# Softcap attention and a maxout MLP: the multiply by the softmax reciprocals of quads 5 to 23, on VectorE in one operation in place of two on GpSimd

## The chip, the cores and the metric

One Trainium2 chip, one core. The time is that of the device for one execution, in microseconds (us), lower is better. A core has five engines with queues of their own, each in order: TensorE (PE, with its weight loads as PEld), VectorE (DVE), ScalarE (ACT), GpSimd (POOL) and SyncE (SP), which here issues almost all DMAs. Engines wait for each other through semaphores. SBUF is the working memory, PSUM takes the results of matmuls.

## The reference

Attention with a soft cap for 8 batches, 12 heads, 448 positions and head size 64, then a layer that takes the larger of two projections, and an output projection. Inputs and output are fp32.

```python
scores = (1 / np.sqrt(64)) * np.matmul(q, k.transpose(0, 1, 3, 2))
scores = cap * np.tanh(scores / cap)                     # cap = 30
attn = np.exp(scores - np.max(scores, axis=-1, keepdims=True))
attn = attn / (np.sum(attn, axis=-1, keepdims=True) + 1e-09)
x = np.matmul(attn, v)                                   # [8, 12, 448, 64]
x = x.transpose(0, 2, 1, 3).reshape(8 * 448, 768)
out = np.maximum(x @ w1, x @ w2) @ w_out                 # w1, w2: 768x1024, w_out: 1024x768
```

## The kernel before

**Attention.** The work is cut into pairs of heads (48, six to a batch) and *quads* of two pairs (24, `t` = 0 to 23 in the main loop). Keys lie across the partitions, so the scores come out transposed: for each quad PE makes 14 score matmuls (`scores`, L295 and L290), ACT makes tanh (L296, L298) and exp (L303, `ex`). No maximum is subtracted; the cap bounds the scores. `pv` (L339, L353) multiplies by v for one pair and accumulates in the PSUM tile pv, of which there is one buffer; VectorE copies it to U (L356, four buffers, one per quad). For the sums over keys VectorE first adds the parts of exp (esum: `add`, L322, L324, L326), from quad 5 on, and PE sums over partitions with a matrix of ones (L352) into ss, copied to st (L359).

**The reciprocals.** They go round through DRAM, to be turned and copied to all partitions. For quad t: SP stores the sums (`sums<-st`, L362) right after pv of the second pair of quad t; VectorE takes the reciprocal (`invert`, L368) and SP writes it to DRAM (`rec_d<-rec_s`, L370) one quad later; SP reads it back for 64 partitions at a time (`spread`, `rec_b<-rec_d`, L376, two DMAs, two buffers) two quads later. `normalize` (L388) then multiplies U by rec_b, an operation for each pair on GpSimd, and writes bf16 to xT, which holds two batches.

**The MLP.** The larger of two projections is computed as relu(x @ (w1 - w2)) + x @ w2; the second part is multiplied through beforehand (wm = w2 @ w_out). `moe(b)` is a generator for one batch. PE makes eight groups of six matmuls (L401), each into a buffer of the PSUM tile mm (two buffers for all of this work); VectorE drains each with a relu to gT (L405). Then come output halves of 14 matmuls (L413 with wm, L416 with w_out), drained to osb (L420) and stored by SP (L431, L436, L440, L423). `F(n)` takes n matmuls out of the queue `fill_q`, to fill PE between attention's matmuls. In the first quads the queue holds the preparation of the weights; moe(0) is appended in quad 4, moe(1) to moe(6) in quads 8, 11, 14, 17, 20 and 23, and moe(7) after the loop.

**Order.** All of it is written by hand: an engine runs its instructions in the order in which the program issues them. In quad t of the loop, from quad 5 on, the order around `normalize` is: scores and exp for quad t+1, filling, `cross` (a DMA that transposes q and k of three pairs, `qkT<-kqf`, L268, in two of three quads), `spread(t - 2)`, loads of q, k and v; `pv(t, 0)`, filling; **`normalize(t - 2)`**; more scores, esum additions and filling; `invert(t - 1)`, loads; the last scores of t+1; `pv(t, 1)` with its copies and the store of the sums. GpSimd's other work in the loop is to cast the loaded q, k and v (L178 to L190, L158, L163). After the loop there are `invert`, `spread` and `normalize` for the last two quads between stretches of filling.

The lines of the helper that the quads call:

Of the kernel before, what the change touches and what calls it, by code (L numbers as in the profile page):

```python
# [10 lines left out]
def kernel(  # L11
# [11 lines left out]
    nc = tc.nc  # L23
# [14 lines left out]
    NQ = N // 2  # L38
# [174 lines left out]
    def subtract(c):  # L213
        nc.vector.tensor_sub(wd_sb[:, c, :], w1_in[c], w2b[:, c, :])
# [35 lines left out]
    def transposes(i):  # L250

        g, n = divmod(i, L)
        ps = mm_psum.tile([P, 512], f32, name="mm").bitcast(bf16)
        x = flat(g)[:, n, :]

        todo = [(j * D, (j % 3) * P + (j // 3) * 64) for j in range(6)]
        odd = i // NP % 2
        todo += [(Q0 + j * D, Q0 + (64 * j if not odd else 0 if j == 6 else 64 + 64 * j)) for j in range(R7)]
        for c, to in todo:
            for a in range(2):  # L260
                r = slice(64 * a, 64 * a + 64)
                nc.tensor.transpose(ps[r, to : to + 64], x[r, c : c + D], ident[r, r])
        nc.tensor.transpose(ps[:, NJ * P : Q0], x[:, NJ * P : Q0], ident)
        nc.vector.tensor_copy(qkT_of(g)[:, n, :, :].rearrange("p j c -> p (j c)")[:, : Q0 + S], ps[:, : Q0 + S])  # L264

    def cross(g):

        nc.sync.dma_start_transpose(  # L268
            out=qkT_of(g).rearrange("p n j c -> p (n j) c"), in_=kqf[g % 2].rearrange("p n j c -> p (n j c)")
        )  # L270
# [6 lines left out]
    def scores(t, p, m0=0, m1=2):  # L277

        if m0 == 0:
            tanh[t, p] = att.tile([P, 4, S], bf16, name="tanh")  # L280
        if p == 2:
            s = s_psum.tile([P, 2, 512], f32, name="s")
        for m, (ab, j) in list(enumerate(PARTS[p]))[m0:m1]:
            i = 2 * t + ab
            g = i // L
            k0 = qkT[g][:, i % L, :, :].rearrange("p j c -> p (j c)")
            o = Q0 + (64 * (i // NP % 2) if g >= NT else 0)
            qTn = k0[:, o : o + S]
            if p == 2:
                nc.tensor.matmul(s[:, m, :S], k0[:, 3 * P : 4 * P], qTn)  # L290
                continue
            s = s_psum.tile([P, 2, 512], f32, name="s")
            for h in range(2):
                r = slice(64 * h, 64 * h + 64)
                nc.tensor.matmul(s[:, h, :S], k0[r, j * P : (j + 1) * P], qTn[r, :])  # L295
            nc.scalar.activation(tanh[t, p][:, 2 * m : 2 * m + 2, :], s[:, :, :S], AF.Tanh, scale=scale / cap)  # L296
        if p == 2:
            nc.scalar.activation(tanh[t, p][:, 0:2, :], s[:, :, :S], AF.Tanh, scale=scale / cap)  # L298

    def ex(t, p):  # L300
        n = 2 if p == 2 else 4
        expo[t, p] = att.tile([P, n, S], bf16, name=f"expo{p}", bufs=1 if p == 3 else 2)
        nc.scalar.activation(expo[t, p], tanh[t, p][:, 0:n, :], AF.Exp, scale=float(cap))  # L303
# [7 lines left out]
    def add(t, ab, step):  # L311

        if t < NS or t >= NQ:
            return
        if t not in esum:
            esum[t] = att.tile([P, 4, S], bf16, name="esum")
        d = esum[t][:, 2 * ab : 2 * ab + 2, :]
        if step == 2:

            r = slice(64 * ab, 64 * ab + 64)  # L320
            d = esum[t][r, ab::2, :]
            nc.vector.tensor_add(d, d, expo[t, 2][r, :, :])  # L322
        elif step == 0:
            nc.vector.tensor_add(d, e_of(t, ab, 1 if ab else 0), e_of(t, ab, 2 if ab else 1))  # L324
        else:
            nc.vector.tensor_add(d, d, e_of(t, ab, 0 if ab else 2))  # L326

    U, sums, rec, recd = {}, {}, {}, {}
# [37 lines left out]
    def invert(t):  # L366
        r = xpool.tile([32, 56], f32, name="rec_s")
        nc.vector.reciprocal(r, sums[t])  # L368
        recd[t] = dram.tile([32, 56], f32, name="rec_d")
        nc.sync.dma_start(out=recd[t], in_=r)  # L370

    def spread(t):
        rec[t] = xpool.tile([P, 2, S], f32, name="rec_b")
        lines = recd[t].rearrange("(n h a) c -> h n (a c)", h=2, a=8)
        for h in range(2):
            nc.sync.dma_start(  # L376
                out=rec[t][64 * h : 64 * h + 64, :, :], in_=lines[h : h + 1, :, :].to_broadcast([64, 2, S])
            )

    xT = {}  # L380

    def normalize(t, ab, eng=nc.gpsimd):
        i = 2 * t + ab
        b, hp = divmod(i, NP)
        if i % (2 * NP) == 0:
            xT[b // 2] = xpool.tile([P, NP, 2 * S], bf16, name="xT")
        cs = slice((b % 2) * S, (b % 2 + 1) * S)
        eng.tensor_mul(xT[b // 2][:, hp, cs], U[t][:, ab, :], rec[t][:, ab, :])  # L388


    gT = {}
# [52 lines left out]
    def F(n):  # L444
        while n > 0 and fill_q:
            try:
                next(fill_q[0])
                n -= 1
            except StopIteration:
                fill_q.pop(0)  # L450
# [68 lines left out]
    def weights(i):  # L519
        if MS <= i < MS + KC:  # L520
            fill_q.append(turn_w2(i - MS))
        if MS < i <= MS + KC:
            fill_q.append(premultiply(i - MS - 1))

    def extra(i):
        for f, a in todo[i]:
            f(*a)

    for t in range(NQ):
        i = 2 * t  # L530
        more = t + 1 < NQ
        more8 = 1 if t >= 8 and more else 0
        weights(i)
        if t % 3 == 2 and t > 5:
            fill_q.append(moe(t // 3 - 1))
        if more:
            scores(t + 1, 0)
        ex(t, 3)
        F(2)
        if 3 < i <= 3 + KC:  # L540
            subtract(i - 4)
        add(t, 0, 1)
        F(2)
        if i + 3 < NT * L:
            transposes(i + 3)
        if t == 0:
            cast(nc.vector, 0, "v")
        F(4 + more8 if more else 0)
        if t == 4:
            normalize(t - 2, 0)  # L550
            normalize(t - 2, 1)
        if t in crosses:
            cross(crosses[t])
        if t > 4:
            spread(t - 2)
        extra(i)
        F(5 + 2 * more8 if more else 3)
        if more:
            scores(t + 1, 1)
            ex(t + 1, 0)  # L560
        if t > 0:
            pv(t, 0)
        F(4)
        add(t, 1, 0)
        F(3 + more8 if more else 4)
        F(3 if more else 0)
        if 3 <= i < 3 + KC:
            subtract(i - 3)
        if t > 4:
            normalize(t - 2, 0)  # L570
            normalize(t - 2, 1)
        if more:
            scores(t + 1, 2)
            ex(t + 1, 1)
        weights(i + 1)
        if t == 4:
            fill_q.append(moe(0))
        if i + 4 < NT * L:
            transposes(i + 4)
        add(t, 0, 2)  # L580
        F(2 + more8 if more else 2)
        add(t, 1, 2)
        F(4 + more8 if more else 3)
        add(t, 1, 1)
        F(2 if more else 8)
        if 1 < t < 4:
            spread(t - 2)
        if t > 2:
            invert(t - 1)
        extra(i + 1)  # L590
        F(2 + more8 if more else 0)
        if more:
            scores(t + 1, 3)
            ex(t + 1, 2)
        if t == 0:
            pv(t, 0)
        if t == 3:
            spread(t - 1)
        pv(t, 1)
        F(4)  # L600
        if more:
            add(t + 1, 0, 0)
        F(3 if more else 0)
        if 0 < t < 3:
            invert(t - 1)
        if 1 < t < 4:
            normalize(t - 2, 0)
            normalize(t - 2, 1)
    F(6)
    spread(NQ - 2)  # L610
    F(10)
    invert(NQ - 1)
    F(16)
    spread(NQ - 1)
    normalize(NQ - 2, 0)
    normalize(NQ - 2, 1)
    F(30)
    normalize(NQ - 1, 0)
    normalize(NQ - 1, 1)
    fill_q.append(moe(B - 1))  # L620
    F(10 ** 9)
# [33 lines left out]
```

## Time and profile before

| | |
|---|---|
| time, median of 3 runs | 374.17 us (371.63 to 374.65) |
| the profiled execution | 374.65 us, span 372.9 us, PE clock 0.995 |
| busy: PE, ACT, DVE, POOL | 344.8, 281.5, 231.5, 161.5 us |
| L388, the multiplies on POOL | 48, 59.4 us, mean 1258 ns, idle before them 125.5 us |
| DMA | 71.56 MB, mean 192 GB/s |

The span runs from the first to the last instruction. The page cuts it into 40 slices of 9.3 us; a digit is the busy share of a slice in tenths. In lists of waits, "A <- B: x, n, m" says that A's engine stood x us in all, n times and m us at the longest, until B was done. In a timeline row the first number is the start in us and the second how long the row took; in brackets stands the idle time before it and what ended it. SPq is SP issuing a DMA. "x2" are two instructions merged in one row.

### The profile page before, as it was taken

The numbers are of one execution on the slowest core, as the hardware profiler recorded it, in microseconds if no ns is written. First come the engines' busy times: TensorE is split into PE (matmuls) and PEld (weight loads), VectorE is DVE, ScalarE is ACT, GpSimd is POOL, SyncE is SP. The second block draws the span as 40 slices with busy tenths as digits, with TensorE's granted clock in tenths as the row PEclk, the third lists the DMA queues.
The fourth block names the chain that finished last, engine by engine and source line by source line (L and its number), as shares of the span: only waits on it lengthen the run. The fifth ranks groups of instructions, "written<-read, shape, count | busy, mean of one in ns | idle before, by whom it ended". The sixth has DMA issues, their size and how long they took to land.

```text
span 372.9 us, 6501 instructions
## 1 busy us (share of the span) xinstructions
PE 344.8 (92%) x2454; PEld 165.2 (44%) x2454; DVE 231.5 (62%) x389; ACT 281.5 (75%) x265; POOL 161.5 (43%) x197
## 2 busy tenths in 40 slices
PE   4668897999999999999979999999999999999996
PEld 2223444444444444444434344534453445555553
DVE  4153557577886777767674687659767868533421
ACT  4996998899999989998978899988998993000000
POOL 4851168690864376234554554544644332220000
PEclk9999999999999999999998999999999999999999
DMA  7998899768799979999599968897998133512022
GB/s 260 327 241 186 324 274 274 149 145 189 190 238 238 212 188 252 202 209 251 145 230 239 261 189 193 220 235 214 216 261 200 53 92 129 150 45 86 0 86 84
DMA packets 101200, 71.56 MB, mean 192 GB/s; under 512 B 56496, under 2 KB 96176, under 8 KB 101168
## 3 DMA queue, kind: packets, MB, share of 16 engines
q1 hardware_dynamic: 99216, 67.99, 70.6%
q0 software_dynamic: 1952, 3.15, 4.6%
q8 instruction: 19, 0.31, 0.4%
q14 instruction: 13, 0.11, 0.1%
HBM read 53.48 MB, written 11.18 MB: 173 GB/s over the span
## 4 chain that ended last, share of the span: by engine, by line
PE 56%; ACT 15%; DMA 12%; DVE 8%; SPq 5%; issue 2%; POOL 2%; DVEq 0%; POOLq 0%; ACTq 0%
PE mm L416 14%; PE mm L401 12%; PE mm L413 10%; ACT expo L303 7%; ACT tanh L296 7%; PE pv L339 6%; PE s L295 5%; DMA qr<-in_q_dram 4%; DMA kr<-in_k_dram 3%; PE pv L353 3%; DMA qkT<-kqf 2%; PE ss L352 2%; PE mm L232 2%; DMA vr<-in_v_dram 1%; DMA rec_d<-rec_s 1%
## 5 line engine op out<-in xcount | busy, mean ns | idle before, releaser
L303 ACT ACTIVATE expo<-tanh 128x1792 bf16<-128x1792 bf16 (+1 forms) x96 | 144.8, 1509 | 0.1
L296 ACT ACTIVATE tanh<-s 128x896 bf16<-128x896 f32 x144 | 124.2, 915 | 26.1 <-PE s L295 24.6
L388 POOL TENSOR_TENSOR xT<-u,rec_b 128x448 bf16<-128x448 f32 x48 | 59.4, 1258 | 125.5 <-DMA rec_b<-rec_d 81.0
L416 PE MATMUL mm<-wo_sb,gT 128*128 128x384 bf16 x448 | 86.1, 328 | 0.0
L401 PE MATMUL mm<-xT,wd_sb 128*128 128x448 bf16 x384 | 79.3, 352 | 1.0 <-DVE osb L420 0.6
L356 DVE COPY u<-pv 128x448 f32<-128x448 f32 x48 | 30.0, 624 | 72.0 <-PE pv L353 70.5
L413 PE MATMUL mm<-wm_sb,xT 128*128 128x384 bf16 x336 | 67.9, 330 | 0.3 <-DVE gT L405 0.2
L416 PEld LDWEIGHTS <-gT 128*128 128x128 bf16 x448 | 43.6, 98 | 30.5 <-issue 2.9
L295 PE MATMUL s<-qkT 64*128 64x448 bf16 x288 | 43.8, 373 | 10.6 <-ACT tanh L298 3.9
L401 PEld LDWEIGHTS <-wd_sb 128*128 128x128 bf16 x384 | 37.0, 98 | 36.2 <-issue 4.5
L420 DVE COPY osb<-mm 128x384 f32<-128x384 f32 x56 | 30.9, 553 | 32.8 <-PE mm L416 32.3
L405 DVE TENSOR_SCALAR gT<-mm 128x448 bf16<-128x448 f32 x64 | 39.3, 617 | 11.5 <-PE mm L401 11.2
L413 PEld LDWEIGHTS <-xT 128*128 128x128 bf16 x336 | 32.9, 99 | 24.4 <-issue 3.4
L339 PE MATMUL pv<-expo,vp 128*64 128x448 bf16 x288 | 37.5, 370 | 0.7 <-DVE u L356 0.7
L322 DVE TENSOR_TENSOR esum<-esum,expo 64x896 bf16<-64x896 bf16 x38 | 29.1, 766 | 0.7
L326 DVE TENSOR_TENSOR esum<-esum,expo 128x896 bf16<-128x896 bf16 x38 | 28.3, 744 | 1.6
L324 DVE TENSOR_TENSOR esum<-expo 128x896 bf16<-128x896 bf16 x38 | 28.8, 757 | 0.0
L295 PEld LDWEIGHTS <-qkT 64*128 64x128 bf16 x288 | 9.6, 95 | 37.5 <-issue 29.5
L298 ACT ACTIVATE tanh<-s 128x896 bf16<-128x896 f32 x24 | 22.0, 916 | 2.5 <-PE s L290 1.9
L232 PE MATMUL mm<-wo_sb,w2T 128*128 128x384 bf16 x96 | 18.5, 326 | 4.7 <-DVE qkT L264 4.3
L339 PEld LDWEIGHTS <-vp 128*64 128x64 bf16 x288 | 12.6, 110 | 21.5 <-issue 16.7
L178 POOL CAST kqf<-kr 128x1152 bf16<-128x1152 f32 x12 | 16.1, 1342 | 5.3 <-DMA kr<-in_k_dram 4.4
(59 smaller groups left out, 246.9 us busy)
## 6 DMA issues: line engine op xcount, KB each, us to landing
rec_b<-rec_d SPq DMA_DIRECT2D x48, 224.0 KB
kr<-in_k_dram SPq DMA_DIRECT2D x12, 576.0 KB
qr<-in_q_dram SPq DMA_DIRECT2D x12, 576.0 KB
vr<-in_v_dram SPq DMA_DIRECT2D x12, 576.0 KB
out_dram<-osb SPq DMA_DIRECT2D x17, 384.0 KB
out_dram<-osb SPq DMA_DIRECT2D x22, 192.0 KB
osb<-in_moe_w_dram SPq DMA_DIRECT2D x6, 512.0 KB
vr<-in_v_dram SPq DMA_DIRECT2D x4, 672.0 KB
```

What stands on the lines that cost most here:

```text
L295: nc.tensor.matmul(s[:, h, :S], k0[r, j * P : (j + 1) * P], qTn[r, :])
L296: nc.scalar.activation(tanh[t, p][:, 2 * m : 2 * m + 2, :], s[:, :, :S], AF.Tanh, scale=scale / cap)
L303: nc.scalar.activation(expo[t, p], tanh[t, p][:, 0:n, :], AF.Exp, scale=float(cap))
L322: nc.vector.tensor_add(d, d, expo[t, 2][r, :, :])
L339: nc.tensor.matmul(ps[r, :S], vp[g % 2][:, 2 * n + h, j, :], e_of(t, ab, j)[:, h, :], start=(j == 0), stop=False)
L356: nc.vector.tensor_copy(U[t][:, ab, :], ps[:, :S])
L388: eng.tensor_mul(xT[b // 2][:, hp, cs], U[t][:, ab, :], rec[t][:, ab, :])
L401: nc.tensor.matmul(ps[:, :S], wd_sb[:, c, f * P : (f + 1) * P], x[:, c, cs], start=(c == 0), stop=(c == KC - 1))
L405: nc.vector.tensor_relu(g[:, f, cs], ps[:, :S])
L413: nc.tensor.matmul(ps[:, : DM // 2], x[:, c, ts], wm_sb[:, c, hs], start=(c == 0), stop=False)
L416: nc.tensor.matmul(ps[:, : DM // 2], g[:, f, ts], wo_sb[:, f, hs], start=False, stop=(f == FC - 1))
L420: nc.vector.tensor_copy(osb[:, hs], ps[:, : DM // 2])
```

## The change

`normalize` takes a whole quad. For quads 0 to 4 it makes the same two multiplies on GpSimd, at the same places. For quads 5 to 23 it makes one multiply on VectorE, over both pairs (128 partitions, 2x448). For t of 7 and more its place in the loop moves from behind `pv(t, 0)` to behind the last scores of quad t+1, ahead of `pv(t, 1)`. After the loop the multiplies of the last two quads stand behind 14 and 38 matmuls of filling after the last spread, in place of none and 30. PE, ACT and SP have the same instructions in the same order; only VectorE (19 more) and GpSimd (38 fewer) differ.

```diff
-    def normalize(t, ab, eng=nc.gpsimd):
-        i = 2 * t + ab
+    def normalize(t):
+        i = 2 * t
         b, hp = divmod(i, NP)
         if i % (2 * NP) == 0:
             xT[b // 2] = xpool.tile([P, NP, 2 * S], bf16, name="xT")
         cs = slice((b % 2) * S, (b % 2 + 1) * S)
-        eng.tensor_mul(xT[b // 2][:, hp, cs], U[t][:, ab, :], rec[t][:, ab, :])
+        if t < 5:
+            for ab in range(2):
+                nc.gpsimd.tensor_mul(xT[b // 2][:, hp + ab, cs], U[t][:, ab, :], rec[t][:, ab, :])
+        else:
+            nc.vector.tensor_mul(xT[b // 2][:, hp : hp + 2, cs], U[t], rec[t])
...
         if t == 4:
-            normalize(t - 2, 0)
-            normalize(t - 2, 1)
+            normalize(t - 2)
...
-        if t > 4:
-            normalize(t - 2, 0)
-            normalize(t - 2, 1)
+        if 4 < t < 7:
+            normalize(t - 2)
         if more:
             scores(t + 1, 2)
             ex(t + 1, 1)
...
         if more:
             scores(t + 1, 3)
             ex(t + 1, 2)
+        if t > 6:
+            normalize(t - 2)
         if t == 0:
             pv(t, 0)
...
         if 1 < t < 4:
-            normalize(t - 2, 0)
-            normalize(t - 2, 1)
+            normalize(t - 2)
...
     F(16)
     spread(NQ - 1)
-    normalize(NQ - 2, 0)
-    normalize(NQ - 2, 1)
-    F(30)
-    normalize(NQ - 1, 0)
-    normalize(NQ - 1, 1)
+    F(14)
+    normalize(NQ - 2)
+    F(24)
+    normalize(NQ - 1)
     fill_q.append(moe(B - 1))
     F(10 ** 9)
```

## The prediction

> **What bounds the kernel now.** I read the page's busy times and its 40 slices, then the busy time by stage, the list of waits, the rows of single tiles, and the timeline around one quad.
>
> ```profile
> PE 344.8 (92%) x2454; PEld 165.2 (44%) x2454; DVE 231.5 (62%) x389; ACT 281.5 (75%) x265; POOL 161.5 (43%) x197
> PE   4668897999999999999979999999999999999996
> DVE  4153557577886777767674687659767868533421
> ```
>
> PE is full from the ninth slice (some 80 us) to the end, and VectorE is two thirds busy. By stage:
>
> ```profile
> 90.00:200.00 110.00, 106.22 (x672) 48.67 (x670) 78.12 (x127) 101.71 (x96) 57.56 (x64) 0.98 0.91 219
> 200.00:285.00 85.00, 84.11 (x538) 38.55 (x537) 62.00 (x102) 79.01 (x75) 38.92 (x47) 1.00 0.92 219
> ```
>
> Columns after the length: PE, weight loads, DVE, ACT, POOL, clock, DMA share, GB/s. Between 90 and 285 us PE works 190.3 of 195 us, ACT 180.7, DVE 140.1, and the DMA engines are at 0.91 of their time. So any stall given to PE there ends up in the total; there are only about 4 us of PE idle left to win. Then the waits (total, times, longest):
>
> ```profile
> POOL xT L388 <- DMA rec_b<-rec_d: 81.0, 16, 9.1
> DVE u L356 <- PE pv L353: 70.5, 45, 3.5
> ...
> PE s L295 <- DMA qkT<-kqf: 2.5, 2, 2.3
> ...
> PE mm L401 <- DVE osb L420: 0.6, 1, 0.6
> ```
>
> GpSimd waits 81 us for the spread reciprocals (rec_b), and nobody minds. PE hardly ever waits for VectorE: VectorE waits for PE. The timeline at quad t=12, where the multiply of quad 10 will stand:
>
> ```profile
> 178.59 0.49 DVE L368 RECIPROCAL rec_s<-sums 32x56 f32<-32x56 f32 x1 [0.15 <-DMA sums<-st]
> 179.48 0.62 DVE L356 COPY u<-pv 128x448 f32<-128x448 f32 x1 [0.40 <-PE pv L353]
> 180.03 0.61 DVE L359 COPY st<-ss 128x448 f32<-128x448 f32 x1
> 181.22 0.54 DVE L420 COPY osb<-mm 128x384 f32<-128x384 f32 x1
> ```
> ```profile
> 180.20 1.31 SPq L376 DMA_DIRECT2D rec_b<-rec_d  x2
> 184.98 1.10 SPq L370 DMA_DIRECT2D rec_d<-rec_s  x1
> 186.19 0.60 SPq L362 DMA_DIRECT2D sums<-st  x1
> 187.27 4.28 SPq L268 DMA_TRANSPOSE qkT<-kqf  x1
> 191.65 1.28 SPq L376 DMA_DIRECT2D rec_b<-rec_d  x2
> ```
> ```profile
> 184.96 2.61 POOL L388 TENSOR_TENSOR xT<-u,rec_b 128x448 bf16<-128x448 f32 x2 [4.13 <-DMA rec_b<-rec_d]
> ```
>
> VectorE is past the reciprocal at 179.08, at the place where the new multiply is queued. But rec_b of quad 10 is issued only at 180.20 and lands at 184.96. SP's queue runs late: between 100 and 285 us its gaps of over 0.2 us add up to some 25 us, most of them waits for rec_d to land, and one transpose takes it 4.28 us.
>
> **What the Trainium skill says.** "VectorE: DVE Perf Modes", The perf-mode tier table: an fp32 tensor_tensor has the 1x mode only, so joining the two pairs saves one instruction's start, not element time. The trace agrees: these bf16 additions take 0.61 us at least for 896 elements, the fp32 L214 (below) 1.15 for 1,024. "SBUF — State Buffer", SBUF: two separate sides: a VectorE operation with two SBUF inputs and a GpSimd operation that reads SBUF take the shared port from each other for the whole instruction. The trace fits it: L324, two SBUF inputs, takes 0.612 us at best and 1.576 at worst. "Perfetto Trace Analysis", DVE / Act Engine Instruction: an instruction stays in its engine's wait queue until its semaphores are there; the trace shows the queue kept in order, so what stands behind a waiting one waits too.
>
> **The change part by part.** *Removed:* 38 GpSimd multiplies of quads 5 to 23. At 1.26 us they are 48 us of a GpSimd that nobody waits for. GpSimd's casts of q and k no longer stand behind that wait; but at quad 12 they ended at 180.83 and their transpose was issued at 187.27, because SP was late, so an earlier cast brings little. What GpSimd took from VectorE's additions goes in part (L322: mean 766 ns, median 623, 38 of them, some 5 us), but PE doesn't wait for these: nothing.
>
> *Added:* 19 VectorE multiplies of 128x896 fp32. No row has that shape. The nearest is
>
> ```profile
> L214 DVE TENSOR_TENSOR wd_sb<-osb,gT x6: 1148/1264/2104, 44.0 to 76.2; 128x1024 bf16<-128x1024 f32 x6
> ```
>
> (minimum, median, maximum in ns): 1.148 less 128 elements at that page's 0.96 GHz is 1.015 us. The skill's price in the first page above, (N+151)/0.96 ns, gives 1.09 as the upper end; a GpSimd cast in the way can add up to 1.2 us (GpSimd casts a third of the time). I take 1.02, alone: 19.4 us on VectorE, which rises from 0.72 to about 0.79 of the stage. It does not become the bound.
>
> *Moved, with a new wait:* this is what decides. The order of PE, ACT and SP stays as it is and no DMA is moved; the multiply leaves GpSimd's queue for VectorE's. For t = 7 to 23 the multiply of quad t-2 stands on VectorE between the reciprocal of quad t-1 and the copy of U for the second pair of quad t. Behind it are that copy, the copy of the sums (st), an esum addition, and the drains of mm to gT or osb. PE waits for the drains: mm has two buffers, so PE may end two groups and then stands. I lay the landing of rec_b (start of GpSimd's multiply in the trace) beside the end of the reciprocal. VectorE would wait, for t = 7 to 20: 3.4, 0.5, 2.6, 4.2, 4.3, 5.9, 5.5, 1.5, 1.8, 4.2, 4.3, 3.4, 2.7, 3.9 us; for t = 21, 22, 23 the landing is earlier, 0. The two multiplies after the loop: landings 322.65 and 327.6, their places in the queue after the fourth and eighth relu, at 324.6 and 329.1: no wait, and the 1.02 us go into VectorE's gaps.
>
> For each quad I then pushed the queued VectorE rows back by that wait plus 1.02 us, end to end, and compared each drain's new end with the start of the matmul group two further on. At t=12: the multiply would end at 185.98, U at 186.6, st at 187.2, the addition at 187.9, the osb drain at 188.3; PE's group that needs that buffer began at 182.96 (L413): 5.3 us late. The same for t = 7 to 20: 1.7, 0.6, 1.2, 1.1, 3.9, 5.3, 2.5, 1.1, 0.4, 2.8, 3.7, 2.9, 0.7, 3.2, together 31 us.
>
> These don't simply add, since a stall of PE gives SP time to catch up. How much is the one unknown. *Lower end:* SP goes on as before while PE stands; each stall counts only where it exceeds the lateness collected so far. At t=13 PE's wait for qkT of 2.27 us (192.43 to 194.71) disappears in the lateness, and SP is put back to PE's pace once, at 223.2 to 225.3, where it waits for an osb drain. Sum, for t = 7, 11, 12, the qkT wait, 16 and 17: 1.7 + 2.1 + 1.5 - 2.3 + 2.8 + 0.9 = 6.7 us. *Upper end:* SP is held too. The store of the sums (L362) waits for st, which is behind the multiply: st would end 2.2 us after rec_b lands. Against the old issue of L362 that is late by 1.9 us at t=7, then 0.8, 1.8, 1.0, 2.7, 1.3, 0.3, 0.8 and 2.7 (t = 9, 10, 12, 13, 15, 16, 18, 19), and the next transpose and the next rec_b stand behind it. So SP slips with PE, and the waits return in full: the ledger then ends at 16.4 us. What reduces it is SP's own slack: 2.8 to 4.0 us waits for rec_d in the quads without a transpose, and DMA issues that took 1 to 2.5 us in place of 0.6. With the DMA engines at 0.91 SP recovers little, so I take 12 us, somewhat over the middle of 6.7 and 16.4.
>
> Sum: profiled execution 374.65 us (span 372.9) + 12 = 386.65; that execution is 0.48 above the median of 374.17, so **386.2 us**.
>
> **The rivals.** *SP catches up wholly:* VectorE's wait is a one-time shift, as the lower end, and the casts freed on GpSimd shorten SP further: +2 to +7, some 379 us. For it: SP waits for PE or VectorE only at 224 us in that stretch. Against it: L362 behind st. *GpSimd was the cause of SP's lateness (faster):* casts of kr start right after the multiply (187.65 after 187.57), the transposes wait for casts, and rec_b stands behind the transposes. If freed casts bring rec_b forward by more than VectorE's wait (4 us at the typical quad; the deciding point is landing before the reciprocal's end), the waits vanish and the PE gaps after 90 us go (0.49, 0.26, 0.27, 2.27, 0.57): 374.17 - 3.9 = 370.3. Against it: at quads 12 and 13 SP reached the transposes 5 to 6 us after the casts. *Only the operation counts:* landings in time, the 1.02 us at t=8, 14, 15 cost 0.5 each: 375.5. *Every wait in full:* 374 + 31 = 405, if PE's delay slows SP one for one everywhere; SP's own waits for rec_d speak against it.
>
> **How the numbers follow.** Forecast, PE held by VectorE's wait with SP partly slipping (381 to 394): 0.68. SP catches up (376 to 381): 0.12. Operation only: 0.09. Faster rival: 0.06. In full: 0.05. A measurement tells about 1% from no change here. Faster by over 1%: 0.05; within: 0.09; slower: 0.86. Range 376 to 396: it leaves out the faster rival, half of the operation-only case and the full sum.
>
> **What would show it.** Right: the VectorE multiply's rows with idle time before them ended by the rec_b DMA, 30 to 50 us in all; PE's groups (L405, L417 and L420 in the new line numbers) waiting for VectorE's drains, in place of the 0.6 us of now; L362 issued within 0.1 us of st's end; the stage from 90 to 285 us about 12 us longer and the tail after 320 unchanged. Wrong: rec_b landing before the reciprocal ends at most quads, or PE without new gaps, or a multiply far from 1.02 us.

## The result, and the profile after

The changed kernel takes 388.54 us in the median of 4 runs (388.0 to 389.42), against 373.88 us of the kernel before beside it (371.63 to 374.65): a ratio of 1.0405, with a 95% interval of 1.0354 to 1.0456. The profiled execution took 388.07 us with a span of 386.3, 13.4 us more than the 372.9 of before. Ratios leave out executions more than 1.5% above the fastest of their kernel; the executions profiled in experiments 7 and 8 are among those left out.

The line numbers move: the VectorE multiply is L392, GpSimd's are L390, PE's groups L405 (was L401), L417 (was L413) and L420 (was L416), the relu drain L409, the osb drain L424. First the page: busy times, slices of PE, clock and VectorE, and the chain's shares by engine and by line; below it, from the page of before, the clock and the chain. PEclk is the clock that PE was granted, in tenths of full speed.

```profile
PE 348.5 (90%) x2454; PEld 166.0 (43%) x2454; DVE 246.5 (64%) x408; ACT 281.6 (73%) x265; POOL 115.8 (30%) x159
...
PE   4669997899998999977999999889996999999996
...
DVE  4164566677785968646868684869686678652421
...
PEclk9999999999999999996999999999998999999999
...
PE 34%; DMA 28%; DVE 13%; SPq 12%; ACT 5%; issue 4%; POOL 3%; DVEq 0%; POOLq 0%; ACTq 0%
PE mm L405 9%; DMA rec_b<-rec_d 8%; PE mm L420 7%; DMA qr<-in_q_dram 7%; DMA rec_d<-rec_s 7%; PE mm L417 6%; SPq L268 5%; DMA kr<-in_k_dram 4%; SPq L376 3%; PE pv L339 3%; DMA vr<-in_v_dram 3%; PE s L295 3%; DVE xT L392 2%; DVE esum L324 2%; ACT expo L303 2%
```
```profile
PEclk9999999999999999999998999999999999999999
...
PE 56%; ACT 15%; DMA 12%; DVE 8%; SPq 5%; issue 2%; POOL 2%; DVEq 0%; POOLq 0%; ACTq 0%
```

VectorE gained 15.0 us of work and GpSimd lost 45.7. VectorE is at 64%, so it has not become an engine without slack. PE does the same 2,454 matmuls, and its row shows what the change cost: 3.7 us more busy time (348.5 against 344.8) and 9.7 us more idle time (386.3 - 348.5 = 37.8, against 372.9 - 344.8 = 28.1). The two make the 13.4 us. The chain (the work that ended last, followed back from the end) tells the same in another way: before, PE held 56% of it, DMA 12% and SP's queue 5%; now 34%, 28% and 12%. PE still has the largest share, but the way of the reciprocals through DRAM has moved into the chain: of DMA's 28%, 8 are rec_b and 7 rec_d (before, none and 1); most of the rest are loads of q, k and v. The list of waits names the new ones (total, times, longest):

```profile
ACT tanh L296 <- PE s L295: 36.7, 31, 7.3
...
DVE xT L392 <- DMA rec_b<-rec_d: 25.6, 11, 5.4
...
PE mm L405 <- DVE gT L409: 8.4, 6, 4.5
...
PE mm L405 <- DVE osb L424: 2.8, 2, 1.5
...
PE mm L417 <- DVE osb L424: 2.4, 2, 1.5
```

Read it from below. PE stands 13.6 us for VectorE's drains; before it was 0.6. VectorE stands 25.6 us for rec_b. GpSimd stood 81.0 us for it before, and no one waited for GpSimd. ScalarE's wait for scores (24.6 us before) grew as well: what PE loses, its customers wait for. The 2.5 us that PE stood for qkT have gone from the list. The longest stall in the timeline, at t=11, first VectorE:

```profile
167.58 0.48 DVE L368 RECIPROCAL rec_s<-sums 32x56 f32<-32x56 f32 x1
173.42 1.09 DVE L392 TENSOR_TENSOR xT<-u,rec_b 128x896 bf16<-128x896 f32 x1 [5.36 <-DMA rec_b<-rec_d]
174.43 0.62 DVE L356 COPY u<-pv 128x448 f32<-128x448 f32 x1
174.96 0.61 DVE L359 COPY st<-ss 128x448 f32<-128x448 f32 x1
175.49 0.61 DVE L409 TENSOR_SCALAR gT<-mm 128x448 bf16<-128x448 f32 x1
```

then PE, and SP's queue:

```profile
171.27 0.36 PE L405 MATMUL mm<-xT,wd_sb 128*128 128x448 bf16 x1
176.16 5.08 PE L405 MATMUL mm<-xT,wd_sb 128*128 128x448 bf16 x14 [4.53 <-DVE gT L409]
```
```profile
164.26 4.35 SPq L268 DMA_TRANSPOSE qkT<-kqf  x1
168.70 1.34 SPq L376 DMA_DIRECT2D rec_b<-rec_d  x2
```

The whole mechanism is in these nine rows. SP is held by the transpose until 168.6, issues rec_b at 168.7, and it is there at 173.42. VectorE's queue has reached the multiply at 168.06. Behind it stand two copies and a relu, none of which needs rec_b. The relu is the drain that frees the mm buffer for PE's next group, which would have gone on at 171.63 and starts at 176.16, 4.53 us later.

### The profile page after: what moved, and what is told of

Read it like the earlier page. It is cut to its first block, busy times and chain, and to the rows that moved or that the text cites. A ratio compares the mean times of both kernels' runs of the same rounds, so it can differ in the third digit from the quotient of the medians.

```text
span 386.3 us, 6452 instructions
## 1 busy us (share of the span) xinstructions
PE 348.5 (90%) x2454; PEld 166.0 (43%) x2454; DVE 246.5 (64%) x408; ACT 281.6 (73%) x265; POOL 115.8 (30%) x159
## 4 chain that ended last, share of the span: by engine, by line
PE 34%; DMA 28%; DVE 13%; SPq 12%; ACT 5%; issue 4%; POOL 3%; DVEq 0%; POOLq 0%; ACTq 0%
PE mm L405 9%; DMA rec_b<-rec_d 8%; PE mm L420 7%; DMA qr<-in_q_dram 7%; DMA rec_d<-rec_s 7%; PE mm L417 6%; SPq L268 5%; DMA kr<-in_k_dram 4%; SPq L376 3%; PE pv L339 3%; DMA vr<-in_v_dram 3%; PE s L295 3%; DVE xT L392 2%; DVE esum L324 2%; ACT expo L303 2%
## 5 line engine op out<-in xcount | busy, mean ns | idle before, releaser
L405 PE MATMUL mm<-xT,wd_sb 128*128 128x448 bf16 x384 | 83.5, 364 | 11.2 <-DVE gT L409 8.4
L420 PE MATMUL mm<-wo_sb,gT 128*128 128x384 bf16 x448 | 85.3, 326 | 0.0
L417 PE MATMUL mm<-wm_sb,xT 128*128 128x384 bf16 x336 | 66.9, 326 | 3.0 <-DVE osb L424 2.4
L405 PEld LDWEIGHTS <-wd_sb 128*128 128x128 bf16 x384 | 37.9, 100 | 49.0 <-issue 19.3
L420 PEld LDWEIGHTS <-gT 128*128 128x128 bf16 x448 | 43.3, 98 | 30.0 <-issue 2.2
L424 DVE COPY osb<-mm 128x384 f32<-128x384 f32 x56 | 30.9, 551 | 26.2 <-PE mm L420 26.0
L409 DVE TENSOR_SCALAR gT<-mm 128x448 bf16<-128x448 f32 x64 | 39.3, 616 | 12.1 <-PE mm L405 11.8
L417 PEld LDWEIGHTS <-xT 128*128 128x128 bf16 x336 | 32.5, 98 | 26.8 <-issue 5.5
L158 POOL CAST vp<-vr 128x1152 bf16<-128x1152 f32 x12 | 13.9, 1158 | 99.1 <-DMA vr<-in_v_dram 91.8
L392 DVE TENSOR_TENSOR xT<-u,rec_b 128x896 bf16<-128x896 f32 x19 | 20.3, 1070 | 25.6 <-DMA rec_b<-rec_d 25.6
L324 DVE TENSOR_TENSOR esum<-expo 128x896 bf16<-128x896 bf16 x38 | 31.6, 833 | 0.0
L326 DVE TENSOR_TENSOR esum<-esum,expo 128x896 bf16<-128x896 bf16 x38 | 26.8, 705 | 1.6
L322 DVE TENSOR_TENSOR esum<-esum,expo 64x896 bf16<-64x896 bf16 x38 | 23.6, 621 | 0.7
```

Source lines behind the costliest of these rows:

```text
L392: nc.vector.tensor_mul(xT[b // 2][:, hp : hp + 2, cs], U[t], rec[t])
L405: nc.tensor.matmul(ps[:, :S], wd_sb[:, c, f * P : (f + 1) * P], x[:, c, cs], start=(c == 0), stop=(c == KC - 1))
L409: nc.vector.tensor_relu(g[:, f, cs], ps[:, :S])
L417: nc.tensor.matmul(ps[:, : DM // 2], x[:, c, ts], wm_sb[:, c, hs], start=(c == 0), stop=False)
L420: nc.tensor.matmul(ps[:, : DM // 2], g[:, f, ts], wo_sb[:, f, hs], start=False, stop=(f == FC - 1))
L424: nc.vector.tensor_copy(osb[:, hs], ps[:, : DM // 2])
```

## The experiments

Ratios are to the kernel before, run beside each. The diffs are against the changed kernel. The theory: the engine matters, not the place or the operation; VectorE waits for rec_b with PE's drains behind it. Rivals: the 19 operations cost the time themselves, or the new place does; and later, that it lies in the store of the sums or in SP's order.

**1. The new places, on GpSimd.** 

> The new places, but all multiplies on GpSimd, one per pair. Theory (VectorE's wait for rec_b costs the time): the wait is GpSimd's again, PE without new gaps, within 1% of before, 371 to 377 us. Rival 'the place' (a later multiply delays what reads xT): some 380 to 388 us. Rival 'the VectorE work and the shared port': also about as before, so this run tells place from engine only.

```diff
-        if t < 5:
-            for ab in range(2):
-                nc.gpsimd.tensor_mul(...)
-        else:
-            nc.vector.tensor_mul(xT[b // 2][:, hp : hp + 2, cs], U[t], rec[t])
+        for ab in range(2):
+            nc.gpsimd.tensor_mul(...)
```

373.03 us, ratio 0.9999 (0.9978 to 1.0019). The waits of this kernel:

```profile
POOL xT L389 <- DMA rec_b<-rec_d: 99.4, 20, 8.9
```

GpSimd waits 99 us and it costs nothing. So the place is harmless, the few matmuls moved after the loop included.

**2. The operations without the wait.** 

> The changed kernel, but the VectorE multiply of quads 5 to 23 takes U twice, in place of U and rec_b: the reciprocals of these quads are left out of the result, their DMAs stay. The same 19 operations of 128x896 fp32 at the same place, without the wait for rec_b. Theory: the operations alone cost little, 373 to 377 us, VectorE idle ahead of them near 0, PE stalls for its drains under 2 us in all. Rival 'the operations or the shared port cost it': 384 to 389 us, as the changed kernel.

```diff
-            nc.vector.tensor_mul(xT[b // 2][:, hp : hp + 2, cs], U[t], rec[t])
+            nc.vector.tensor_mul(xT[b // 2][:, hp : hp + 2, cs], U[t], U[t])
```

370.97 us, ratio 0.9937 (0.991 to 0.9965). The rows of tile xT (minimum, median, maximum in ns; first and last start):

```profile
L392 DVE TENSOR_TENSOR xT<-u x19: 1015/1016/1084, 114.7 to 324.7; 128x896 bf16<-128x896 f32 x19
```

The same 19 operations at the same places, without the read of rec_b, cost nothing; the kernel is even 2.4 us faster than before. This is close to the 370.3 us of the rival in which the waits vanish: PE has neither the qkT wait of before nor any time at half clock (mean clock 1.000, against 0.995).

**3. VectorE at the old place**, 4 to 5 us earlier in the quad. 

> The changed kernel with the VectorE multiply at the place of before, behind pv of the first pair, some 4 to 5 us earlier in VectorE's queue. Theory: the wait for rec_b grows by about that each time, to 60 us or more in all, and the time to 398 to 415 us. Rival 'the operations cost it, wherever they stand': 386 to 390 us. Rival 'SP slips with PE one for one': well above 415 us.

```diff
-        if 4 < t < 7:
+        if t > 4:
             normalize(t - 2)
...
-        if t > 6:
-            normalize(t - 2)
```

433.74 us, ratio 1.1632 (1.1543 to 1.1722): well beyond the 398 to 415 us that were expected, and in the range of the rival in which SP slips with PE one for one, though VectorE's wait (45.5 us) is smaller than the 60 that were expected. Its waits, and SP's:

```profile
DVE xT L392 <- DMA rec_b<-rec_d: 45.5, 14, 6.2
...
PE ss L352 <- DVE esum L322: 18.6, 14, 4.2
...
PE mm L405 <- DVE osb L424: 13.6, 3, 6.5
```
```profile
SPq L370 <- DVE rec_s L368: 54.7, 17, 9.6
```

Here the multiply of quad t-2 stands ahead of the reciprocal of quad t-1, so, as the trace reads, the wait goes round in a ring: rec_b late, multiply late, the next reciprocal late, its store (L370) late with SP held meanwhile (54.7 us, against 20.2), the next rec_b late. In the timeline the multiplies of two quads start 15.4 us apart, each behind such a wait:

```profile
218.62 1.09 DVE L392 TENSOR_TENSOR xT<-u,rec_b 128x896 bf16<-128x896 f32 x1 [2.92 <-DMA rec_b<-rec_d]
...
221.47 0.48 DVE L368 RECIPROCAL rec_s<-sums 32x56 f32<-32x56 f32 x1
...
234.03 1.09 DVE L392 TENSOR_TENSOR xT<-u,rec_b 128x896 bf16<-128x896 f32 x1 [2.73 <-DMA rec_b<-rec_d]
...
238.06 0.48 DVE L368 RECIPROCAL rec_s<-sums 32x56 f32<-32x56 f32 x1
```

VectorE's longest single wait (6.2 us) is little above that of the changed kernel (5.4), yet the quads are longer throughout: from t=7 to 21 the reciprocals come 16.3 us apart, 12.9 before. In the changed kernel the reciprocal goes first. No run here breaks the ring by itself, so it stays a reading. And a third of the loss is not waiting: PE's idle time grows by 39.1 us and its busy time by 19.1, as its clock is halved for 37.6 us of the loop.

**4. VectorE half a quad later**, ahead of the first pv of the next quad. 

> The changed kernel with the VectorE multiply of quad t-3 ahead of pv of the first pair of quad t (for quad 5 at the start of quad 8), about half a quad or 6 us later than in the change. Theory: rec_b has landed at most places, VectorE's wait falls from 26 us to under 6, and the time to 373 to 379 us. Rival 'the operations cost it': 386 to 390 us.

```diff
+        if t > 8:
+            normalize(t - 3)
         pv(t, 0)
...
-        if t > 6:
-            normalize(t - 2)
```

(The multiply for t = 8 stands at the start of its quad, that of quad NQ-3 ahead of the first filling after the loop.) 372.49 us, ratio 0.9968 (0.9944 to 0.9991). VectorE has no listed wait for rec_b, and PE waits for its drains 1.6 us in all. This version is faster than both kernels, by 0.3% against before. PE has 75% of the chain, against 56% before and 34% in the changed kernel:

```profile
PE 75%; ACT 8%; DMA 7%; DVE 7%; issue 1%; SPq 1%; POOL 0%; DVEq 0%; ACTq 0%
```

**5. Behind the second pair's copies**, 1.2 us later, so that st and the store of the sums (L362) no longer stand behind the multiply. 

> The changed kernel with the VectorE multiply one step later: behind the copies of U and st of the second pair, ahead of the esum addition and the drains. VectorE reaches it 1.2 us later, so it still waits for rec_b, but SP's store of the sums (L362) no longer stands behind that wait. Theory (a good half of the cost came back because SP was held through st): SP keeps its pace, L362 again issued well after st's end, 377 to 382 us. Rival (only the drains behind the wait matter, SP's slip does not): the 1.2 us come off at most of the eight or so stalls and no more, 383 to 387 us.

```diff
-        if t > 6:
-            normalize(t - 2)
...
         pv(t, 1)
+        if t > 6:
+            normalize(t - 2)
```

387.03 us, ratio 1.0346 (1.0286 to 1.0406): the theory that the late store is what makes SP slip fell; the rival's 387 us are just reached. SP's idle time ahead of L362 between 95 and 305 us went from 19.8 us in the changed kernel to 9.4 (1.8 before), but the time stayed. The waits are now

```profile
PE mm L405 <- DVE gT L409: 9.4, 7, 2.7
...
DVE xT L392 <- DMA rec_b<-rec_d: 8.7, 5, 2.5
```

and PE still stands some 14.5 us for drains (ten gaps of 0.26 to 2.72 us), as these, and an esum addition, are queued behind the multiply as before. Of these 14.5 us, 4.4 fall in four quads in which the multiply did not wait at all, 1.93 of them behind one that took 2.04 us beside GpSimd's casts; experiment 2 has 1.2 us in these quads. So close ahead of the drains the operation may cost something by itself. SP slips as it did: rec_b is issued 4.9 us later than before at t=14 and 14.9 at t=23, against 5.4 and 13.2 in the changed kernel. The store of the sums alone is not the link; which other is was not settled.

**6. At the end of the quad**, 2.5 to 3 us later. 

> The changed kernel with the VectorE multiply at the end of quad t, behind pv of the second pair, its copies, the next esum addition and seven matmuls of filling: some 2.5 to 3 us later than in the change, and ahead of most of the drains no more. Theory (how late rec_b is at VectorE's place sets the cost, with half a quad later at 372.5 us and the changed place at 388.5): only the longest waits are left, 1 to 3 us at some five quads, 375 to 381 us. Rival (the cost is of any wait on VectorE's queue, whatever its length): 384 us or more.

```diff
-        if t > 6:
-            normalize(t - 2)
...
-        if 1 < t < 4:
+        if 1 < t < 4 or t > 6:
             normalize(t - 2)
```

376.05 us, ratio 1.0078 (1.0046 to 1.0111).

```profile
PE mm L405 <- DVE gT L409: 5.1, 6, 1.5
...
DVE xT L392 <- DMA rec_b<-rec_d: 2.2, 4, 0.8
```

The wait for rec_b is nearly used up and no stretch of the loop runs at half clock; some drains still come late behind the multiply. By place, on VectorE: 433.7 us (4 to 5 us earlier), 388.5, 387.0 (1.2 later), 376.05 (2.5 to 3 later), 372.5 (half a quad later). The later the place, the less it costs, as it would if rec_b landed at about the same point of each quad; but the first value has the ring in it, and experiment 5 the drains close behind, so this is no curve of one cause.

**7. The reciprocals' DMAs on GpSimd's queue**, so that rec_b isn't behind SP's transposes. 

> The changed kernel, but GpSimd issues the three DMAs of the reciprocals (rec_d and both of rec_b) in place of SP, at the same points of the program. Theory (rec_b is late because SP's queue is late): rec_b lands earlier, VectorE's wait falls under 10 us in all, 372 to 379 us. Rival (GpSimd's queue is as late, since its casts wait for v): the wait stays at 20 us or more and the time at 384 us or more, with the transposes late too.

```diff
-        nc.sync.dma_start(out=recd[t], in_=r)
+        nc.gpsimd.dma_start(out=recd[t], in_=r)
...
-            nc.sync.dma_start(
+            nc.gpsimd.dma_start(
```

386.19 us (382.67 to 395.98; 384.23 for the three in the ratio), ratio 1.0293 (1.021 to 1.0377), as the rival had it. The rows are of the execution of 395.98 us:

```profile
POOL rec_d L370 <- DVE rec_s L368: 82.9, 18, 14.4
POOL rec_b L376 <- DMA rec_d<-rec_s: 81.3, 21, 8.5
...
DVE xT L392 <- DMA rec_b<-rec_d: 23.4, 8, 7.5
...
PE s L295 <- DMA qkT<-kqf: 6.9, 1, 6.9
```

The wait only moves to another queue. GpSimd's is in order too: it stands 82.9 us for the reciprocals and 81.3 until rec_d has landed, and its casts of q and k stand behind that. The casts for the transpose that PE waited for ended at 154.8 us (147.7 in the changed kernel). But that transpose also held SP for 8.2 us, where those of the changed kernel took 3.6 to 5.0; why was not settled.

**8. Both: half a quad later, and the DMAs on GpSimd.** 

> The multiply half a quad later, as in the run of that name, and the three DMAs of the reciprocals issued by GpSimd. If SP's lateness is the only thing left, transposes come earlier and it gains 1 to 3 us on that run: 369 to 372 us. If GpSimd's queue is held by its waits for v and k, casts and rec_b come late: 374 us or more.

 The edits are those of 4 and 7. 387.19 us (382.11 to 389.31), ratio 1.0267 (1.018 to 1.0354), where 4 alone gave 0.9968. The ratio rests on two executions, of 382.11 and 385.97 us: slower than the kernel of 4, but by how much is only roughly known. The rows are of one of 388.42 us:

```profile
POOL rec_b L376 <- DMA rec_d<-rec_s: 79.7, 21, 8.3
...
PE s L295 <- DMA qkT<-kqf: 5.0, 3, 4.2
DVE xT L392 <- DMA rec_b<-rec_d: 4.9, 1, 4.9
...
PE mm L405 <- DVE xT L392: 3.5, 1, 3.5
```

At the place where VectorE had no wait in 4, it now has one of 4.9 us, and PE stands 3.5 us for that multiply beside the 5.0 us for qkT. So on GpSimd's queue the transposes come later, and once rec_b too.

**9. rec_b ahead of the transpose on SP.** 

> The changed kernel with SP's order turned in the quads that transpose: rec_b is issued ahead of the transpose of q and k, not behind it. Theory (rec_b is late because of what stands ahead of it in SP's queue): in two of three quads rec_b lands 1 to 4 us earlier, since SP then has to wait for rec_d first, and VectorE's wait falls by a third or more; but the transpose starts 1.3 to 4 us later, and at every second transpose qkT landed just in time, so PE waits for qkT: 378 to 390 us, with the stalls for drains under 7 us and the wait for qkT over 3 us. Rival (rec_b's place in SP's queue doesn't matter): VectorE's wait and PE's stalls for drains as in the change.

```diff
-        if t in crosses:
-            cross(crosses[t])
...
         spread(t - 2)
+        if t in crosses:
+            cross(crosses[t])
```

391.16 us, ratio 1.0478 (1.0419 to 1.0536), a little above the 378 to 390 us of the theory. VectorE's wait for rec_b falls as meant, from 25.6 us to 15.0, and a new wait, for qkT, takes the room; PE's stalls for drains fall to 10.3 us only, where under 7 were expected:

```profile
DVE xT L392 <- DMA rec_b<-rec_d: 15.0, 8, 4.7
...
PE mm L417 <- DVE osb L424: 6.3, 2, 4.4
...
PE s L295 <- DMA qkT<-kqf: 5.3, 3, 2.4
...
PE mm L420 <- DVE gT L409: 3.0, 1, 3.0
```

The transpose now stands behind rec_b's own wait for rec_d in SP's queue (42.6 us in all, against 24.3); and in the quads where a wait for rec_b is left, one stall of PE is as long as in the changed kernel (4.4 us, with half clock behind it).

**10. VectorE from quad 12 on only.** 

> The change for quads 12 to 23 alone; quads 5 to 11 stay on GpSimd, at the place of before. Theory (each late stretch is paid again, SP slipping with PE): the stalls from t=14 on remain, which in the changed kernel made up some 3 to 4 of the 13 us by the shift of U's copies after t=13; with SP at its old lateness there the first late quads (16, 17, 20) cost their 3 us each: 378 to 384 us. Rival (a one-time shift of PE against SP, as large wherever it starts): some 388 us. Rival (only the first quads cost): under 376 us.

```diff
-        if t < 5:
+        if t < 12:
...
-        if 4 < t < 7:
+        if 4 < t < 14:
...
-        if t > 6:
+        if t > 13:
```

384.86 us (380.59 to 386.15), ratio 1.0303 (1.0231 to 1.0376). That is just above the 378 to 384 us of the theory and 3 us below the rival of a one-time shift, from which its interval does not part it (it ends at 1.0376, that of the change begins at 1.0354). The times refute only that the first quads alone cost. The trace, of the fastest execution (380.59 us), says more:

```profile
DVE xT L392 <- DMA rec_b<-rec_d: 9.5, 5, 3.9
...
PE mm L405 <- DVE gT L409: 5.2, 5, 1.9
```

PE stalls behind the multiply of t=14 (1.87 us), of t=16 (1.96) and of t=20 (1.81 and 0.54), at t=16 and 20 with half clock behind, and the second pair's copy of U falls behind that of before step by step: 1.8 us at t=16, 4.4 at t=20, 6.4 at t=23. So here the loss is paid again at each late quad and not as one shift. Twelve of the 19 quads cost some three quarters (0.0303 of 0.0405), which the intervals do not tell from their share.

## Why the prediction was right, and where it was off

386.2 us were predicted and 388.54 measured: slower, by the mechanism named, 2.3 us off. That VectorE's wait for rec_b, with PE's drains behind it, is the cause, experiments 1 and 2 show; the closeness of the number is in part luck, as the terms below show.

**The multiply's own cost: nothing, as taken.** Experiment 2 shows it. Its size was slightly low. Tile xT of the changed kernel:

```profile
L392 DVE TENSOR_TENSOR xT<-u,rec_b x19: 1015/1092/1093, 119.0 to 342.5; 128x896 bf16<-128x896 f32 x19
```

The 1.015 us that were worked out from L214 come true right behind the reciprocal (1.015 to 1.024, once 1.056); behind a wait it is the upper end, 1.09, the price in "VectorE: DVE Perf Modes", under The TRN2 errata. The mean is 1,070 ns in place of 1,020.

**VectorE's wait: right in kind, below the 30 to 50 us.** By quad, from the end of the reciprocal to the start of the multiply, it came out at 3.7, 0, 1.3, 3.5, 5.4, 0, 1.0, 1.1, 0.9, 3.4, 1.6, 0, 1.0 and 3.9 us for t = 7 to 20. The first quads are close to the list in the prediction, and from t=12 on most are smaller, which is SP catching up while VectorE and PE are delayed: at t=12 rec_b is issued 2.0 us later than before, the second pair's copy of U ends 9.9 us later. But it catches up in part only: against before, the issue of rec_b was late by 0.5 us at t=7, 3.9 at t=11, 5.0 to 5.5 for t = 14 to 19 and 13.2 at t=23. As predicted there is no wait after the loop.

**PE's stalls: the kind right, 8 of 14 places, the sum near.** By quad, PE stood 1.3, 0.3, 0.9, 4.5, 0.6, 1.5, 1.5 and 3.0 us for drains at t = 7, 8, 10, 11, 14, 16, 17 and 20. At the other six quads of the list it had no such gap, not even at t=12, right after the longest stall, where 5.3 us were listed. 13.6 us of gaps for drains, less 0.57 of before, less the qkT waits of before (2.27 and 0.27), make 10.5 us. L362 was issued within 0.03 us of st's end at the nine quads named (and at t=20, which that list leaves out though its working gives some 3 us there). That this is what holds SP, on which the upper end was built, isn't borne out: experiment 5 took half of that waiting away and the time stayed. So of the two reasons for 12 us between 6.7 and 16.4 one doesn't carry, and a choice inside so wide a range that comes within 1.5 us of the stalls is luck. (SP's gaps of before add up to 21.7 us in the trace, not 25; no term of the sum rests on that.)

**What the sum left out: PE at half clock.** The slices of the clock have a 6 and an 8, before one 8. The stretches, in the table by stage (columns as in the prediction, the clock behind POOL):

```profile
174.00:180.80 6.80, 4.64 (x13) 1.87 (x13) 5.23 (x8) 0.56 (x1) 4.07 (x6) 0.50 1.12 291
180.80:190.00 9.20, 9.20 (x61) 4.11 (x60) 7.31 (x13) 7.83 (x8) 1.90 (x3) 1.00 0.65 170
...
296.80:300.30 3.50, 3.20 (x10) 1.15 (x8) 2.48 (x4) 0.00 (x0) 1.67 (x3) 0.51 0.40 125
```

From within the stall of 4.53 us on PE is at half clock until 180.8, behind one of 2.66 us for 3.4 us. Half of the 7.8 us that PE was busy there is lost, 3.9; before there was one such stretch of 3.4 us (behind the qkT wait), worth 1.7. The net 2.2 us are the larger part of PE's 3.7 us more of busy time. With the 10.5 us of stalls this makes 12.7 of the span's 13.4; PE's other idle time is 0.8 us less and its other busy time 1.5 us more, which wasn't placed (0.7 us were there by t=4, ahead of the first changed instruction). What failed is thus a missing term: a stall was priced at its length, and a long one can cost more. The stalls came out 1.5 us under the 12, and the 2.2 us of half clock made up for it. "TensorE: Matmul & The Clock Gate" states this under Part 1: The HAM clock gate: PE's default is half clock, after about 3.4 us of idle time, and about 3.4 us of sustained work release it. The lengths here agree (3.4 us, and twice that), but the stalls of 2.27 and 2.66 us that set it off are shorter than the page's window; the measurement decides.

The length of a stall alone does not set half clock off: in experiment 5 a stall of 2.72 us had no half clock behind it, in experiment 10 stalls of 1.96 and 1.81 us had. In all twelve traces the changes of clock lie, from the first on, on a grid of 3.413 us; cut into windows by that grid, each of the 20 full-clock windows in which PE stood idle for 1.97 us or more was followed by one at half clock, none of the 1,144 with 1.62 us or less, and 4 of the 9 between. The 2.72 us of experiment 5 lay across two windows, 1.49 and 1.23; the 4.53 us of the changed kernel too, 2.33 and 2.20, and so cost two windows.

**The rivals.** That only the operation counts, and that GpSimd was the cause of SP's lateness, both lacked the same thing: rec_b in time. Freed casts bring it forward, but not by enough: in experiment 4, where GpSimd is as free and VectorE doesn't wait, rec_b is issued at most 3.2 us earlier against the second pair's copy of U (t=12, where 5.9 were needed), 1.7 at t=11 and not at all at t=16, where 4.3 and 4.2 were needed. With the wait removed (experiment 2) and with the place moved (4), the kernel is indeed 0.6% and 0.3% faster than before. The full sum of 405 failed to come because six of its 14 stalls did not. The forecast's stage is right too: the second pair's copy of U is 0.7 us late at t=4, 3.9 at t=7, 10.3 at t=13 (6.5 at t=14, where before had its own qkT wait and half clock), 12.0 at t=20, 13.8 at t=23, and from there on the tail is shifted as a whole.

## What to carry to other kernels

Before an operation goes to another engine, lay the landing of its slowest operand beside the time at which that engine's queue gets to the place, and then name what is queued behind it: the same wait for rec_b was free for 99 us on GpSimd and cost some 14 us at 26 us on the engine that drains PSUM for PE. If the operand is late, move the operation later (half a quad turned 1.0405 into 0.9968); moving the DMA to another in-order queue or ahead of its neighbour made something else late here. Keep it behind the operation on the same engine that its next operand starts from (here the reciprocal), or the wait may feed itself, as the trace of experiment 3 reads. And price a stall of about 2 us or more of a full PE with 3.4 us at half clock behind it: here this followed wherever 2 us of idle time fell into one window of the clock's grid.

## What the runs showed of the hardware

A stall of 2.27 us was enough for PE to run at half clock for 3.4 us behind it, one of 2.66 us likewise, and one of 4.53 us for 6.8 us in all, part of them within the stall; stalls of 1.5 us and less, alone, had none behind them in the changed kernel. Over the twelve traces the clock changed only on a grid of 3.413 us, and went to half for the next window after every full-clock window with 1.97 us or more of PE idle time (20 of 20), never after one with 1.62 us or less (0 of 1,144). The 128x896 multiply took 1.015 to 1.056 us right behind a reciprocal in the changed kernel, 1.09 behind a wait, and once, in experiment 5, 2.04 beside GpSimd's casts.
